# Asking for three summary spreads on ScalarE's queue instead of SyncE's, in a fused block attention and MLP kernel

## Chip, cores, metric

The kernel runs on one core of one Trainium2 chip. The metric is the device time of one execution in microseconds. Before the change it is 621.44 us, the median of three runs (621.18 to 622.95).

## What is computed

Attention over a window and over block summaries, then a two-layer MLP, all in float32:

```python
block, window = (32, 16)
k_sum = k.reshape(B, H, nb, block, D).max(axis=3)
v_sum = v.reshape(B, H, nb, block, D).mean(axis=3)
scores_l = scale * q @ k^T, kept where |i - j| < window
scores_s = scale * q @ k_sum^T + log(block)
a = softmax over both together
x = a @ concat(v, v_sum)
h = x @ w_in
out = (h * erf(softplus(h))) @ w_out
```

q, k and v are 4 batches x 8 heads x 768 positions x 64; w_in is 512 x 2048, w_out 2048 x 512.

## The kernel before

**Tiling.** The 3072 tokens go in 6 chunks of 512. A chunk's attention is done in four quads, one for each pair of heads. A quad has 8 blocks of 64 query positions, and each block sees 96 keys of its window and 24 summaries of its batch, 120 columns in all. So the tile of values of a quad has 120 rows: rows 0 to 95 hold the window's values, and rows 96 to 119 the 24 summary values, the same for all 8 blocks.

**Parts of a quad.** `scores` multiplies queries by keys and summary keys; `softmax` takes the maximum, the exponentials (ScalarE, L606) and the norm (L626, on ScalarE for the fourth quad); `transp` turns the probabilities on TensorE (L637) and ScalarE copies them back into the tile ptr (L642); `av` multiplies them with the tile of values (L663, the value product); `xsplit` stores the result as a high part xh (a cast, L278) and a low part xl (VectorE, L679).

**The MLP.** `mm1` (L766) multiplies xh and xl by a block of w_in that was split in the same way: a cast on ScalarE (L278, "w<-a"), the low part on VectorE (L353). Ahead of that `convert` puts together the raw block rw in three VectorE steps (L331, L334, L337), the first of which needs the block's transfer to have landed. The first quads of the first chunk use the blocks in their order: rw_298 is the first block of w_in, rw_362 the second, and then a third and a fourth; two blocks of w_out follow. `mm2` is the second layer (L917, L921).

**The first chunk.** The first four quads belong to one batch, so its summary values are computed once: `vsum_first` sums the values on TensorE (L502), and ScalarE copies the sums into the tile vsum (L505). From there the 24 rows must be spread over rows 96 to 119 of each quad's tile of values, vwf, 8 times over. For the first quad ScalarE does this with a copy (L278, "vwf<-vsum"). For the other three it is a transfer (L510, "vwf<-vsum", 24 x 8 x 128), which this text calls the first, second and third spread; they serve the second, third and fourth quad. Rows 0 to 95 come from memory (L493, "vwf<-v_win"), the window transfers.

**What sets the order.** Every operation is entered in a `Plan` with its engine, an estimated time, and what it reads and writes. `order` sorts the operations with due times and a long table of corrections (TUNE), and the program emits them in that order; each engine then runs its own instructions strictly one after the other, and waits at the first whose inputs are not there. Before the change SyncE asks for every load and spread.

**Counters.** The arrival of transfers is counted on eight counters, DMAHW0 to DMAHW7 in the rows below. They are dealt out in turn to the transfers as these are written in the program, whatever engine asks, and a transfer is asked for only when the one before it on the same counter has landed.

Of the kernel before, what the change touches and what calls it, by code (L numbers as in the profile page):

```python
# [23 lines left out]
NP = H // 2  # L24
T = 512
SB = S // 64
NB = T // 64
NI = NB // 2
NT = T // 128
NS = 24  # L30
LW = 96
NK = LW + NS
# [19 lines left out]
def f32(ap):  # L52
    return ap.bitcast(F32)
# [127 lines left out]
def bfloat16(x):  # L181

    n = np.array([x], np.float32).view(np.uint32)
    return float(((n + 0x8000) & 0xFFFF0000).astype(np.uint32).view(np.float32)[0])
# [3 lines left out]
def block_attention_mlp(ctx: ExitStack, tc: tile.TileContext, q_t, k_nat, k_win, v_tok, v_nat, v_win, w_in, w_out, out):  # L188
    nc = tc.nc
# [7 lines left out]
    def sb(shape, dtype, name, tag=None):  # L197

        n = math.prod(shape[1:])
        if n % 128 == 0:  # L200
            return pool.tile(shape, dtype, name=name, tag=tag or name)
        t = pool.tile([128, -(-n // 128) * 128], dtype, name=name, tag=tag or name)[0:shape[0], 0:n]
        return t if len(shape) == 2 else t.rearrange("p (a b) -> p a b", a=shape[1]) if len(shape) == 3 else t.rearrange("p (a b c) -> p a b c", a=shape[1], b=shape[2])

    def ps(name, tag):
        return psum.tile([128, 512], F32, name=name, tag=tag)
# [28 lines left out]
    for i in range(3):  # L235
        c = bfloat16(rest)
# [20 lines left out]
    vsum = sb([NK, NP, 128], F32, "vsum")  # L257
# [7 lines left out]
    def pe(us, fn, r=(), w=(), **kw):  # L265
        return P.add({"PE": us}, lambda e: fn(), r, w, **kw)

    def on(us, fn, r=(), w=(), **kw):
        return P.add(us, lambda e: fn(engines[e]), r, w, **kw)

    def act(us, fn, r=(), w=(), **kw):
        return P.add({"ACT": us}, lambda e: fn(), r, w, **kw)

    def dma(kb, fn, r=(), w=(), hold=2.0, **kw):
        return P.add({"SP": max(0.45, kb / 350.0)}, lambda e: fn(), r, w, hold=hold, **kw)

    def copy(e, o, i):
        e.copy(o, i) if e is nc.scalar else e.tensor_copy(o, i)  # L278
# [5 lines left out]
    units = [(kind, g, r) for kind, g in UNITS for r in range(2)]  # L284
    tiles, raws, whl, w32, wide = {}, {}, {}, {}, {}
# [8 lines left out]
    def slot(n, shape, dtype, name):  # L294
        return sb(shape, dtype, name, f"w{n}")
# [7 lines left out]
    def frees(n):  # L303

        return [f"w{n}"] + [f"a{2 * g + r}" for g, x in WHOLE.items() if x == n for r in range(2)]
# [11 lines left out]
    def convert(u):  # L317

        w, s, m = f"w{raw_slot(u)}", {}, number(u)
        at_once = u[0] == "i" or u[1] >= NN  # L320
        home = f"gl{u[2]}" if at_once else f"a{m}"

        def a():
            if at_once:
                s["t"] = sb([128, 2, 512], F32, "a32", home)
            else:
                if u[2] == 0:
                    wide[u[1]] = slot(WHOLE[u[1]], [128, 2, 2, 512], F32, "a32s")
                s["t"] = w32[u] = wide[u[1]][:, u[2]]
            s["a"], s["rw"] = s["t"].bitcast(U32), raws.pop(u)  # L330
            nc.vector.tensor_scalar(s["a"], s["rw"][..., 1], 3, 0x3FFFFFFF, op0=ALU.logical_shift_left, op1=ALU.bitwise_and)  # L331

        def b():
            nc.vector.scalar_tensor_tensor(s["a"], s["rw"][..., 0], 29, s["a"], op0=ALU.logical_shift_right, op1=ALU.bitwise_or)  # L334

        def c():
            nc.vector.scalar_tensor_tensor(s["a"], s["rw"][..., 1], 0xC0000000, s["a"], op0=ALU.bitwise_and, op1=ALU.bitwise_or)  # L337

        on({"DVE": 0.6}, lambda e: a(), [w], [home] if at_once or u[2] else frees(WHOLE[u[1]]))
        on({"DVE": 1.13}, lambda e: b(), [w, home], [home])  # L340
        on({"DVE": 1.13}, lambda e: c(), [w, home], [home])
        if at_once:
            split(u, m if u[0] == "i" else FIRST[m], home, lambda: s["t"])

    def split(u, n, home, whole):
        def high(e):
            t = slot(n, [128, 2, 2, 512], F32R, "w")
            whl[u] = t[:, 0], t[:, 1]
            kept[u] = t
            copy(e, whl[u][0], whole())  # L350

        def low(e):
            e.tensor_tensor(whl[u][1], whole(), f32(whl[u][0]), op=ALU.subtract)  # L353
        on({"ACT": 0.94}, high, [home], frees(n))
        on({"DVE": 1.13}, low, [home, f"w{n}"], [f"w{n}"])

    def parts(m, n):
        u = ("o", m // 2, m % 2)
        split(u, n, f"a{m}", lambda: w32[u])
# [111 lines left out]
    kfirst = [kfs[p // 2][:, p % 2] for p in range(NP)]  # L471

    st = {}

    def where(qd):

        ch, p = divmod(qd, NP)
        seqs = {}
        for j in range(NB):
            seqs.setdefault((NB * ch + j) // SB, []).append(j)  # L480
        return ch, p, [(b, slice(js[0], js[-1] + 1)) for b, js in seqs.items()]
# [16 lines left out]
    def vsum_first(bank):  # L498
        def go(t):
            if t == 0:  # L500
                tiles[bank] = ps("vs", bank)
            nc.tensor.matmul(tiles[bank][0:NK], lhsT=pick[:, 20 - 4 * t:140 - 4 * t], rhs=vts[t // 3][:, t % 3], start=(t == 0), stop=(t == 5))  # L502
        for t in range(6):
            pe(0.87, lambda t=t: go(t), [f"vt{t // 3}"], [bank])
        act(0.5, lambda: nc.scalar.copy(vsum[LW:NK], tiles[bank][LW:NK].rearrange("s (p c) -> s p c", p=NP)), [bank], [f"vsum0{p}" for p in range(NP)])  # L505
        for p in range(NP):
            if p == 0:
                on({"DVE": 1.13, "ACT": 0.95}, lambda e: copy(e, st[0]["vw"][LW:NK], vsum[LW:NK, 0:1, :].to_broadcast([NS, NB, 128])), ["vsum00"], ["vwg0"])
            else:
                dma(100, lambda p=p: nc.sync.dma_start(out=st[p]["vw"][LW:NK], in_=vsum[LW:NK, p:p + 1, :].to_broadcast([NS, NB, 128])), [f"vsum0{p}"], [f"vwg{p}"])  # L510


    def load_quad(qd):
# [115 lines left out]
    def transp(qd):  # L629
        s = st[qd]  # L630
        pr = "pr" if qd >= NP else f"pr{qd}"

        def go():
            s["tp"] = [ps(n, n) for n in PA]
            for a in range(2):
                for i in range(NI):
                    nc.tensor.transpose(s["tp"][a][0:NK, i * 128:(i + 1) * 128], s["pr"][:, NI * a + i], ident)  # L637

        def cp():
            s["pt"] = sb([NK, 2, T], F32, "ptr", "pt")  # L640
            for a in range(2):
                nc.scalar.copy(s["pt"][:, a], s["tp"][a][0:NK, 0:T])  # L642
        pe(0.95, go, [pr], PA)
        act(1.1, cp, PA, ["pt"])

# [7 lines left out]
    def av(qd, bank):  # L653
        s = st[qd]
        s["bank"] = bank

        def go():
            xo = s["xo"] = ps("px", bank)
            for j in range(NB):
                o = slice(64 * j, 64 * j + 64)  # L660
                for a in range(2):
                    r = slice(64 * a, 64 * a + 64)
                    nc.tensor.matmul(xo[r, o], lhsT=s["vw"][:, j, r], rhs=s["pt"][:, a, o], start=True, stop=True)  # L663
        pe(1.08, go, ["pt", "vw"] if qd >= NP else ["pt", f"vwf{qd}", f"vwg{qd}"], [bank])
# [304 lines left out]
    for p in range(3):  # L969
        ksum_first(p)  # L970
        scores(p, banks[p])
        softmax(p, banks[p])
    vsum_first("o2")
    ksum_first(3)
    scores(3, banks[3])
# [3 lines left out]
    for p in range(NP):  # L979
        transp(p)  # L980
        av(p, "o2")
        xsplit(p, {"DVE": 0.6, "ACT": 0.48})
        if p:
            for f in range(G):
                mm1(0, f, (p - 1,))
# [29 lines left out]
    def output(n, bank=None):  # L1015
        transp(n)
        av(n, bank or bank_next())
        xsplit(n, xeng)
# [17 lines left out]
    for k in range(NPER):  # L1036
# [27 lines left out]
        elif k < FAST:  # L1064
# [5 lines left out]
            if qa < NQ:  # L1070
                transp(qa)
# [136 lines left out]
```

## Time and profile before

| | |
|---|---|
| median of the runs | 621.44 us |
| the profiled execution | 622.58 us |
| its span | 620.8 us |
| ScalarE busy | 422.3 us, 68% |
| VectorE busy | 424.0 us, 68% |
| DMA, mean over the span | 242 GB/s |
| SyncE's queue (q1) | 36212 packets, 148.95 MB |
| ScalarE's queue (q10) | 576 packets, 0.52 MB |

The span is the time from the first to the last recorded instruction, the profiled execution's own time lies around it. A row of a timeline reads: start, length, engine, line, operation, output<-input, count, and in brackets how long the engine stood idle before it and what released it. SPq and ACTq are the requests for transfers on SyncE's and ScalarE's instruction streams; a request's length is the time the engine needs to describe the transfer, not that of the transfer. A chain of waits is followed back from the last instruction, each time to what released it. In the list of waits, the first name is the operation that waited, the second what it waited for; then the total, the count and the longest.

ScalarE's queue carries only part of the output at the very end: before that, all transfers are SyncE's.

### The profile page before, as it was taken

What the parts mean: (1) busy time and instruction counts of PE and PEld (TensorE: products, weight loads), DVE (VectorE), ACT (ScalarE), POOL (GpSimd) and SP (SyncE); (2) the same over time, 40 slices, a digit from 0 to 9 for tenths busy, and PEclk for the clock granted to TensorE, in tenths of its full rate; (3) what the DMA queues carried; (4) which work ended last, traced back from release to release, by engine and by line L of the source; (5) the groups of instructions that cost most, each with busy time, mean ns of one, the idle gap of its engine ahead of it and who ended that gap; (6) DMA issues with size and microseconds to landing.
All of it is one profiled execution on the core that took longest, in us unless ns stands there. A gap on an engine that the chain in (4) does not pass through costs nothing.

```text
span 620.8 us, 12141 instructions
## 1 busy us (share of the span) xinstructions
PE 612.9 (99%) x4786; PEld 514.4 (83%) x4786; DVE 424.0 (68%) x884; ACT 422.3 (68%) x855; POOL 3.7 (1%) x27
## 2 busy tenths in 40 slices
PE   9999999999999999999999999999999999999997
PEld 5676666888788889989889889899898898899886
DVE  4989999975989886766857646548546556425442
ACT  5869988986879786885866854855756655552450
POOL 2000000000000000000000000000000000000000
PEclk9999999999999999999999999999999999999999
DMA  8999868654784698799767776756786654574612
GB/s 321 256 337 354 287 205 283 250 183 172 247 304 184 236 339 309 244 370 319 240 217 245 234 264 232 257 209 216 266 289 219 225 170 181 210 265 162 246 68 69
DMA packets 36845, 150.25 MB, mean 242 GB/s; under 512 B 3956, under 2 KB 9396, under 8 KB 24244
## 3 DMA queue, kind: packets, MB, share of 16 engines
q1 hardware_dynamic: 36212, 148.95, 69.4%
q8 instruction: 38, 0.62, 0.4%
q10 hardware_dynamic: 576, 0.52, 0.2%
q14 instruction: 19, 0.16, 0.1%
HBM read 124.13 MB, written 23.07 MB: 237 GB/s over the span
## 4 chain that ended last, share of the span: by engine, by line
PE 93%; DMA 6%; SPq 0%; issue 0%; DVE 0%; ACT 0%
PE ops L921 39%; PE hb L807 15%; PE h L766 13%; PE ha L807 11%; PE ops L917 4%; PE px L663 4%; PE pA L566 3%; DMA rw<-w_in 2%; DMA vwf<-vsum 2%; PE pA L637 1%; PE pB L637 1%; DMA vt<-v_tok 1%; PE pB L566 0%; PE vt L460 0%; SPq L485 0%; SPq L486 0%
## 5 line engine op out<-in xcount | busy, mean ns | idle before, releaser
L921 PE MATMUL ops<-w,gh 128*128 128x512 f32 x704 | 232.8, 396 | 0.0
L921 PEld LDWEIGHTS ops<-w,gh 128*128 128x128 f32 x704 | 132.5, 188 | 27.9 <-issue 0.6
L921 PE MATMUL ops<-w,gl 128*128 128x512 f32 x352 | 137.3, 390 | 0.0
L1166 ACT ACT_TABLE_LOAD x87 | 111.6, 1283 | 1.5
L897 DVE TENSOR_TENSOR hc<-wt,hc 128x1024 f32<-128x1024 f32 x44 | 53.3, 1220 | 76.5 <-ACT wt L885 76.5
L766 PE MATMUL h<-xh,w 128*128 128x512 f32 x256 | 88.8, 406 | 0.0
L278 ACT COPY hc<-hb 128x256 f32<-128x256 f32 x61 | 22.7, 373 | 96.2 <-DVE hc L860 47.6
L921 PEld LDWEIGHTS ops<-w,gl 128*128 128x128 f32 x352 | 66.3, 188 | 12.0
L606 ACT ACTIVATE pr<-pr,stats 128x120 f32<-128x120 f32 x160 | 60.9, 383 | 0.2
L766 PEld LDWEIGHTS h<-xh,w 128*128 128x128 f32 x256 | 48.1, 188 | 12.3 <-issue 2.1
L807 PE MATMUL hb<-w,ws 128*128 128x256 f32 x384 | 56.3, 283 | 0.0
L904 DVE TENSOR_TENSOR gl<-hc,gh 128x1024 fp32r<-128x1024 f32 x44 | 53.8, 1222 | 1.6 <-ACT gh L278 0.7
L807 PEld LDWEIGHTS hb<-w,ws 128*128 128x128 f32 x384 | 50.7, 192 | 0.1
L885 ACT ACTIVATE wt<-wt 128x1024 f32<-128x1024 f32 x48 | 50.4, 1061 | 0.4
L766 PE MATMUL h<-xl,w 128*128 128x512 f32 x128 | 49.9, 390 | 0.0
L857 DVE TENSOR_TENSOR hc<-hb,hc 128x256 f32<-128x256 f32 x32 | 13.5, 422 | 37.4 <-PE hb L807 36.4
L278 DVE CAST gh<-hc 128x1024 fp32r<-128x1024 f32 x38 | 26.3, 691 | 18.1 <-PE ops L921 17.1
L873 ACT ACTIVATE wt<-hc 128x1024 f32<-128x1024 f32 x32 | 32.4, 1052 | 0.2
L606 ACT ACTIVATION_READ_ACCUMULATOR pr<-pr,stats 128x1 f32 x160 | 30.0, 187 | 0.0
L917 PE MATMUL ops<-a32s,gw 128*128 128x512 f32 x64 | 29.5, 595 | 0.0
L766 PEld LDWEIGHTS h<-xl,w 128*128 128x128 f32 x128 | 24.1, 188 | 5.6 <-issue 1.2
L807 PE MATMUL ha<-w,ws 128*128 128x256 f32 x192 | 28.3, 283 | 0.0
(162 smaller groups left out, 1033.9 us busy)
## 6 DMA issues: line engine op xcount, KB each, us to landing
w<-dr SPq DMA_DIRECT2D x36, 1024.0 KB
ws<-ds SPq DMA_DIRECT2D x30, 1024.0 KB
kw<-k_win SPq DMA_DIRECT2D x20, 480.0 KB
rw<-w_in SPq DMA_DIRECT2D x8, 1024.0 KB
rw<-w_out SPq DMA_DIRECT2D x8, 1024.0 KB
dr<-w SPq DMA_DIRECT2D x8, 1024.0 KB
ds<-ws SPq DMA_DIRECT2D x8, 1024.0 KB
vw<-v_win SPq DMA_DIRECT2D x20, 384.0 KB
```

Of the source, the lines that this page charges most:

```text
L278: e.copy(o, i) if e is nc.scalar else e.tensor_copy(o, i)
L606: nc.scalar.activation(s["pr"][:, j], s["pr"][:, j] if qd >= MQ else s["sc"][j // NI][:, i * NK:(i + 1) * NK], AF.Exp, scale=-1.0 if qd >= ...
L663: nc.tensor.matmul(xo[r, o], lhsT=s["vw"][:, j, r], rhs=s["pt"][:, a, o], start=True, stop=True)
L766: nc.tensor.matmul(hs[k, f][:, 0:T], lhsT=w[m], rhs=xt[ch, cc][x], start=(cc == 0 and n == 0), stop=(cc == 3 and n == 2))
L807: nc.tensor.matmul(shape, lhsT=w[m], rhs=y[l], start=first and c == 0 and i == 0, stop=c == 1 and i == 2, skip_group_check=True)
L873: nc.scalar.activation(wt[k, n], hc[k, n], AF.Softplus)
L885: act(0.96, lambda n=n: nc.scalar.activation(wt[k, n], wt[k, n], AF.Erf, scale=-1.0 if k < SOFT else 1.0), [s], [s], table=("sig",), after ...
L897: e.tensor_tensor(hc[k, n], wt.pop((k, n)), hc[k, n], op=ALU.mult)
L904: e.tensor_tensor(gs[k, n][1], hc.pop((k, n)), f32(gs[k, n][0]), op=ALU.subtract)
L917: nc.tensor.matmul(os_[ch, t], lhsT=x[0][:, i % 2, t * 128:(t + 1) * 128], rhs=w32["o", g, i // 2][:, i % 2], start=first, stop=last)
L921: nc.tensor.matmul(os_[ch, t], lhsT=x[y][:, i % 2, t * 128:(t + 1) * 128], rhs=w[m], start=first and n == 0, stop=last and n == 2)
L1166: nc.scalar.preload_act_table_set(sets[o["load"]])
```

## The change

The three requests leave SyncE's stream. In the plan an empty operation stands in their place, so that all else is ordered as before. The requests are made on ScalarE: the first behind the copies of the first quad's ptr, the second and third behind the cast of the first block of w_in.

```diff
@@ split()
             copy(e, whl[u][0], whole())
+            if u == units[0]:
+                spread(2)
+                spread(3)
@@ vsum_first()
-        act(0.5, lambda: nc.scalar.copy(vsum[LW:NK], tiles[bank][LW:NK].rearrange("s (p c) -> s p c", p=NP)), [bank], [f"vsum0{p}" for p in range(NP)])
+        def summed():
+            nc.scalar.copy(vsum[LW:NK], tiles[bank][LW:NK].rearrange("s (p c) -> s p c", p=NP))
+            asked.add(0)
+        act(0.5, summed, [bank], [f"vsum0{p}" for p in range(NP)])
...
-                dma(100, lambda p=p: nc.sync.dma_start(out=st[p]["vw"][LW:NK], in_=vsum[LW:NK, p:p + 1, :].to_broadcast([NS, NB, 128])), [f"vsum0{p}"], [f"vwg{p}"])
+
+                dma(100, lambda: None, [f"vsum0{p}"], [f"vwg{p}"])
+
+    def spread(p):
+        assert 0 in asked
+        asked.add(p)
+        nc.scalar.dma_start(out=st[p]["vw"][LW:NK], in_=vsum[LW:NK, p:p + 1, :].to_broadcast([NS, NB, 128]))
@@ transp()
                 nc.scalar.copy(s["pt"][:, a], s["tp"][a][0:NK, 0:T])
+            if qd == 0:
+                spread(1)
```

`asked` only checks, while the program is written, that a spread stands behind the sums and ahead of its use.

SyncE, from the second window transfer on, before the change; rw is a raw block of weights, vwf_124 holds the tiles of values of the first two quads, vwf_125 those of the last two, and in brackets stands what a request waits for:

```order
L493 DMA vwf_124<-v_win 96x1024 [waits DMAHW5_49]
L510 DMA vwf_124<-vsum_109 24x8x128 [waits DMAHW6_49,Activation_49]
L510 DMA vwf_125<-vsum_109 24x8x128 [waits DMAHW7_49]
L314 DMA rw_434<-w_in 128x2048 [waits DMAHW0_49]
L493 DMA vwf_125<-v_win 96x1024 [waits DMAHW1_49]
L314 DMA rw_494<-w_in 128x2048 [waits DMAHW2_49]
L493 DMA vwf_125<-v_win 96x1024 [waits DMAHW3_49]
L510 DMA vwf_125<-vsum_109 24x8x128 [waits DMAHW4_49]
L314 DMA rw_563<-w_out 128x2048 [waits DMAHW5_49,PE_49]
L314 DMA rw_605<-w_out 128x2048 [waits DMAHW6_49,PE_49]
L519 DMA qb_626<-q_t 128x512 [waits DMAHW7_49]
L444 DMA rows_116<-k_nat 128x768 [waits DMAHW0_49]
```

The same stretch with the change, to the second block of w_out:

```order
L497 DMA vwf_124<-v_win 96x1024 [waits DMAHW5_49]
L314 DMA rw_433<-w_in 128x2048 [waits DMAHW6_49]
L497 DMA vwf_125<-v_win 96x1024 [waits DMAHW7_49]
L314 DMA rw_495<-w_in 128x2048 [waits DMAHW0_49]
L497 DMA vwf_125<-v_win 96x1024 [waits DMAHW2_49]
L314 DMA rw_563<-w_out 128x2048 [waits DMAHW3_49,PE_49]
L314 DMA rw_605<-w_out 128x2048 [waits DMAHW4_49,PE_49]
```

The three spreads are gone. The third block of w_in, rw_434 before and rw_433 now, no longer stands behind a request that needs the sums; and since the counters are dealt anew, it has moved from DMAHW0 to DMAHW6.

ScalarE, from the second copy of the first quad's ptr to the copy of the third quad's, before the change; prf are probabilities, xh_482 (xh_483 with the change) is the high part of the second quad's result:

```order
L642 COPY ptr_382<-pB_369 120x512 [waits PE_49]
L606 ACTIVATE prf_123,stats_106<-h0_300,stats_106 128x120 [waits DVE_49]
L606 ACTIVATE prf_123,stats_106<-h0_300,stats_106 128x120 x3
L606 ACTIVATE prf_123,stats_106<-h1_301,stats_106 128x120 x4
L642 COPY ptr_439<-pA_421 120x512 [waits PE_49,Activation_49]
L642 COPY ptr_439<-pB_422 120x512 [waits PE_49]
L278 CAST w_445<-a32_379 128x1024 [waits DMAHW2_49,DVE_49]
L278 CAST xh_482<-px_463 128x512 [waits PE_49]
L642 COPY ptr_491<-pA_452 120x512 [waits Activation_49]
```

And with the change:

```order
L655 COPY ptr_382<-pB_369 120x512 [waits PE_49]
L523 DMA vwf_124<-vsum_109 24x8x128 [waits DMAHW1_49]
L619 ACTIVATE prf_123,stats_106<-h0_300,stats_106 128x120 [waits DVE_49]
L619 ACTIVATE prf_123,stats_106<-h0_300,stats_106 128x120 x3
L619 ACTIVATE prf_123,stats_106<-h1_301,stats_106 128x120 x4
L655 COPY ptr_438<-pA_422 120x512 [waits PE_49,Activation_49]
L655 COPY ptr_438<-pB_423 120x512 [waits PE_49]
L278 CAST w_444<-a32_379 128x1024 [waits DMAHW2_49,DVE_49]
L523 DMA vwf_125<-vsum_109 24x8x128 [waits DMAHW5_49]
L523 DMA vwf_125<-vsum_109 24x8x128 [waits DMAHW6_49]
L278 CAST xh_483<-px_464 128x512 [waits PE_49]
L655 COPY ptr_492<-pA_453 120x512 [waits Activation_49]
```

Three requests came in. The first stands ahead of the exponentials of the fourth quad. The second and third stand between the cast of the first block and the cast of the second quad's xh; they wait for the counters DMAHW5, last used by the second window transfer, and DMAHW6, last used by the third block of w_in.

More of the change, by code (lines that the diff above doesn't have):

```diff
@@ L473, in block_attention_mlp @@
     st = {}
+    asked = set()
     def where(qd):
@@ L657, in go @@
         def go():
+            assert qd >= NP or qd in asked
             xo = s["xo"] = ps("px", bank)
```

## Prediction

> **What bounds the kernel now.** I read the page first, then the chain of waits of the first 60 us, then each engine's timeline there.
>
> ```profile
> PE 612.9 (99%) x4786; PEld 514.4 (83%) x4786; DVE 424.0 (68%) x884; ACT 422.3 (68%) x855; POOL 3.7 (1%) x27
> 9.90 15.35 DMA rw<-w_in
> 25.26 14.56 DMA vwf<-vsum
> 39.97 1.15 PE px L663 x32
> 42.93 8.20 PE h L766 x36
> PEld ops L917 <- issue: 10.3, 43, 0.3
> ```
>
> The first row (busy time by engine) says that TensorE is busy for 99% of the span. The chain (start, length, what) shows where it is not bound by its own work: up to 39.8 us the end hangs on transfers, the second block of w_in (asked for at 9.90, landed at 25.25) and then the third spread (asked for at 25.26, landed at 39.82). From 39.97 on the chain is TensorE alone, and in the list of waits after 43 us TensorE's matmuls don't appear at all; only its weight loads, which run beside them (the last row is the largest: 10.3 us in 43 times). So whatever time the change gains or loses before 43 us arrives at the end undiminished, and nothing later can give it back.
>
> ```profile
> 27.90 1.15 PE L663 MATMUL px<-ptr,vwf 120*64 120x64 f32 x32 [1.05 <-DMA vwf<-vsum]
> 31.05 0.62 PE L766 MATMUL h<-xh,w 128*128 128x512 f32 x2
> 34.01 1.15 PE L663 MATMUL px<-ptr,vwf 120*64 120x64 f32 x32 [0.52 <-ACT prf L626]
> 35.10 0.65 PE L637 MATMUL pA<-ident,prf 128*120 128x128 f32 x4
> 39.97 1.15 PE L663 MATMUL px<-ptr,vwf 120*64 120x64 f32 x32 [1.03 <-DMA vwf<-vsum]
> 43.00 0.39 PE L766 MATMUL h<-xl,w 128*128 128x512 f32 x1
> ```
>
> These are TensorE's rows (in brackets the idle time ahead and what ended it): the value products of the second, third and fourth quad at 27.90, 34.01 and 39.97, idle for 1.05, 0.52 and 1.03 us before them, and between them at 35.10 the fourth quad's transposes. At 31.05 the ninth and tenth matmul of the first layer begin; the tenth, at about 31.3, is the first to read the second quad's xh. The row at 43.00 is the first matmul on the fourth quad's xl, after which nothing waits. Take all three waits away and TensorE wins 2.6 us: that is the most the change could bring.
>
> ```profile
> 20.00:24.00 4.00, 3.55 (x45) 2.29 (x44) 4.00 (x8) 3.95 (x14) 0.00 (x0) 1.00 1.03 248
> 24.00:28.00 4.00, 2.95 (x24) 2.17 (x24) 3.96 (x6) 2.88 (x9) 0.00 (x0) 1.00 1.05 222
> 28.00:32.00 4.00, 4.00 (x46) 3.40 (x46) 2.93 (x6) 2.92 (x6) 0.00 (x0) 1.00 1.02 273
> ```
>
> The stretches (last columns: granted clock 1.00, DMA share, GB/s) show the DMA engines full, 1.02 to 1.05, in all of this stage.
>
> **What the change removes.** SyncE stood still for the summary values:
>
> ```profile
> SPq L510 <- ACT vsum L505: 8.3, 1, 8.3
> 19.95 1.82 SPq L510 DMA_DIRECT2D vwf<-vsum  x2
> 21.82 0.52 SPq L314 DMA_DIRECT2D rw<-w_in  x1
> 27.51 0.80 SPq L314 DMA_DIRECT2D rw<-w_out  x2
> 28.36 0.42 SPq L519 DMA_DIRECT2D qb<-q_t  x1
> 31.91 0.33 SPq L444 DMA_DIRECT2D rows<-k_nat  x1
> 33.78 0.33 SPq L523 DMA_DIRECT2D kw<-k_win  x1
> SPq L523 <- DMA vwf<-v_win: 1.5, 1, 1.5
> 37.80 2.01 SPq L314 DMA_DIRECT2D rw<-w_in  x2
> ```
>
> After 8.3 us of waiting it asked for two spreads (1.82 us) and only then, at 21.82, for the third block of w_in. With the spreads gone that block is asked for at about 11.6 us, ten microseconds sooner (19.95 less the 8.3 of waiting). I give this nothing directly: the engines were full throughout, and the block queued behind the second block (landed 25.25) and the second window transfer. That one is seen in the row at 27.51, whose order row waits for its counter, DMAHW5; the row at 28.36 waits for DMAHW7, the second spread. So two spreads hold the queue for at most 28.36 - 27.51 = 0.85 us, 0.43 each. The real gain of the loads is those 0.85 us, as far as the spreads' bytes don't pass in the same time on the other queue.
>
> **What it adds: a wait on ScalarE.** The order rows show it: the third spread, now on ScalarE, takes counter DMAHW6, whose last user is now the third block of w_in, and waits until that block has landed. The second waits for DMAHW5, the second window transfer. Queued behind both are, in this order, the cast of the second quad's xh, the third quad's ptr copies, the cast of w, the fourth quad's norm, and the rest.
>
> ```profile
> 21.51 0.59 ACT L642 COPY ptr<-pB 120x512 f32<-120x512 f32 x1
> 25.77 1.11 ACT L278 CAST w<-a 128x1024 fp32r<-128x1024 f32 x1
> 29.09 0.59 ACT L278 CAST xh<-px 128x512 fp32r<-128x512 f32 x1 [2.20 <-PE px L663]
> 31.47 2.40 ACT L626 ACTIVATE prf<-prf,stats 128x120 f32<-128x120 f32 x8
> 25.26 0.83 SPq L510 DMA_DIRECT2D vwf<-vsum  x1
> 614.10 0.38 ACTq L947 DMA_DIRECT2D out<-ob  x1
> 31.92 0.69 DVE L331 TENSOR_SCALAR a<-rw 128x1024 uint32<-128x1024 uint32 x1 [1.04 <-DMA rw<-w_in]
> ```
>
> The price of one request: 0.83 us (SyncE's third spread), as 24 x 8 rows need more describing than the 0.38 us of ScalarE's own output request at 614.10; between these I take 0.83, nearest in shape. The first spread goes out after the copy at 21.51, so from 22.10 to 22.95. It shifts the eight exps, the copies and the cast at 25.77 by 0.83, to 26.6; the cast ends at 27.7 and the second quad's product, at 27.90 before, waits for a copy ending at 26.8 and for the window transfer at 27.5. Hidden, but for a few tenths. The second spread waits until 27.5 and goes out by about 28.4; before, ScalarE idled here until 29.09 (2.20 us), which would have covered it.
>
> The third isn't covered. The third block landed at 31.92 (VectorE's row, idle 1.04 until it). When now? With no spread ahead of it: 27.51 + (31.92 - 28.36) = 31.1. With the first two taking their 0.43 each beside it, as before: 31.9. With each taking twice that, up to its 0.83 of issue: 27.51 + 1.66 + 3.56 = 32.7. I take 31.7, near the row that is there, slightly better as the second spread comes in late. Then the request, 0.83, and 0.1 around it: the cast of xh starts at S = 32.6 instead of 29.09, 3.5 us late.
>
> ```profile
> 29.88 0.68 DVE L679 TENSOR_TENSOR xl<-px,xh 128x512 fp32r<-128x512 f32 x1
> 32.53 1.22 DVE L353 TENSOR_TENSOR w<-a,w 128x1024 fp32r<-128x1024 f32 x1
> 34.92 1.23 DVE L337 SCALAR_TENSOR_TENSOR a<-rw,a 128x1024 uint32<-128x1024 uint32 x1
> 37.77 0.69 DVE L331 TENSOR_SCALAR a<-rw 128x1024 uint32<-128x1024 uint32 x1 [1.02 <-DMA rw<-w_in]
> 41.90 0.68 DVE L679 TENSOR_TENSOR xl<-px,xh 128x512 fp32r<-128x512 f32 x1
> 29.57 0.59 ACT L642 COPY ptr<-pA 120x512 f32<-120x512 f32 x1
> 30.52 1.07 ACT L278 CAST w<-a 128x1024 fp32r<-128x1024 f32 x1
> 36.17 1.05 ACT L278 CAST w<-a 128x1024 fp32r<-128x1024 f32 x1 [0.39 <-DVE a L337]
> ```
>
> How that reaches 43.00: VectorE's xl of the second quad (29.88) needs that cast, so 33.25. ScalarE after the cast: copies and w as at 29.09 to 31.47, so the cast of w begins at S + 1.43 = 34.0 and ends at 35.1. VectorE's low part of w (32.53 before) follows at 35.15, 2.62 late; then its three steps keep their spacing (32.53 to 34.92, 2.39, so 37.5; 1.14 more to the xl at 36.06 before, 38.7; 0.61 to the fourth block's first step, 39.3). That step was at 37.77, held there 1.02 us by the fourth block; it is now 1.5 late, and the block has landed. From there to the fourth quad's xl the rows take 41.90 - 37.77 = 4.13: 43.4 instead of 41.9, ending at 44.1, and the matmul of 43.00 starts at 44.2. **+1.2 us.**
>
> TensorE meanwhile: it reaches the second quad's xh at 31.3 and stops until 33.3, goes on with xl at 34.0, and the third quad's product comes at about 35.8 (34.01 before). The fourth quad's norm (31.47 before, 2.40 long) now ends at 37.4, so that its transposes, which began at 35.10, end at about 38; its product comes at 41, since the cast of the third block (36.17 before) waits for VectorE until 38.8 and the ptr copies stand behind it. All of that stays inside the delay of VectorE's row. In one formula: loss = landing of the third block + 0.93 - 31.4, rounded; 31.1 gives +0.6, 32.7 gives +2.2.
>
> **Sum.** -0 (loads, queue full) + 0 (first two requests, covered) + 1.2 (held ScalarE): span 620.8 to 622.0. The profiled execution took 622.58, 1.8 around its span and 1.14 over the median of 621.44; on the median the sum gives 622.6.
>
> **The rule weighed.** The Trainium skill, DMA: Bandwidth & Descriptors, section "Issuing engines are not separate DMA queues", says that requests from several engines run on the same 16 DMA engines and save only the issuing time. The rows agree: with a DMA share of 1.02 to 1.05 there is no free engine to fill, so by it an earlier request brings nothing, as in my sum; were it false, the third block could land well before 31.1 and the loss would turn into the gain of the second rival.
>
> **Rivals.**
> 1. Slower, a small transfer held up by large ones. On SyncE's queue a spread passed in 0.43 us; on ScalarE's its small pieces may have to alternate with the large ones of the loads. Asked for by 22.95, the first spread would then land only when what stands beside it, up to the third block, is through: 31.1 to 31.9 instead of under 27.9. The second quad's product starts at 31.7; without a wait TensorE needs 43.00 - 27.90 - 0.52 - 1.03 = 13.55 us from there to the matmul of 43.00: 45.2, +2.2, median 623.7. It decides once the first spread lands after 30.7 (30.7 + 13.55 = 44.2). For it: the pieces of one spread are 192 short rows against 8 KB rows of w; against it: no row shows it. The Trainium skill, DMA: Bandwidth & Descriptors, "Queues, rings and completion order", states such a round robin by packet; whether a packet is one row or the whole share of an engine, no run here shows.
> 2. Faster, no hold: the third block lands before ScalarE gets there, at 28.4. Then the third window transfer (landed by 33.78, the request that waited for it) and the fourth come up to 0.85 sooner, the waits of 0.52 and 0.85 of 1.03 go: -1.4, median 620.0. Against it: the queue was full, and the block can't overtake what stands ahead of it.
> 3. The change does nothing: the counter waits are met in time and the transfers stay bound by the full engines: 621.4, for which the block would have to land by 30.5.
>
> **How the numbers follow.** Forecast 0.66, rival 1 0.16, rival 2 0.06, rival 3 0.12. A measurement of this kernel tells about 0.3% from no change, 1.9 us. The forecast's own range, +0.6 to +2.2, is above 1.9 in about one case in six (0.11); rival 1 in most (0.13); rival 2 passes -1.9 only with the first wait gone too (0.03, with what I have missed). So slower 0.24, faster 0.03, same 0.73. The range: 2.2 for the upper ends of the forecast and of rival 1, with a few tenths for the median, gives 623.9; below, it takes in half of rival 3, 621.2.
>
> **What would show it.** Right: a wait of ScalarE of about 3 us before the third spread's request, ended by w_in's third block near 31.7; the cast of the second quad's xh near 32.6; TensorE idle about 2 us before 33.3; the matmul of 43.00 at 44.2; the waits of 1.05, 0.52 and 1.03 changed for one. Rival 1: the second quad's product after 30.7, behind a spread. Rival 2: no idle ScalarE there, product of the fourth quad before 39.5. Wrong altogether if TensorE's idle stretch brought its granted clock under 1.00, or if a TensorE wait after 43 us appeared.

## The result, and the profile after

| | before | with the change |
|---|---|---|
| median of the runs beside each other | 621.54 us (621.18 to 623.17) | 629.12 us (627.54 to 630.67) |
| ratio, 95% interval | | 1.0117 [1.0097, 1.0138] |
| profiled execution, and its span | 622.58, 620.8 us | 629.34, 627.6 us |

Slower by 1.2%, above the range. The span grew by 6.8 us, and all of it lies ahead of one row. TensorE's timeline, with the lines moved by the edit (L679 is the value product, L782 the first layer):

```profile
33.46 1.97 PE L679 MATMUL px<-ptr,vwf 120*64 120x64 f32 x32 [5.74 <-issue]
41.83 1.15 PE L679 MATMUL px<-ptr,vwf 120*64 120x64 f32 x32
46.70 1.15 PE L679 MATMUL px<-ptr,vwf 120*64 120x64 f32 x32
49.74 0.39 PE L782 MATMUL h<-xl,w 128*128 128x512 f32 x1
```

The second quad's product comes at 33.46 instead of 27.90 (+5.56), behind an idle stretch of 5.74 us; the two later products no longer wait; and the matmul that stood at 43.00, ahead of which the fourth quad's xl is made, stands at 49.74 (+6.74). From the second quad's product to it, TensorE needs 16.28 us, where the prediction had 13.55 of work. So **+6.74 = 5.56 late - 1.55 of later waits gone (0.52 + 1.03) + 2.73 of slower work.** The last term is seen in the stretches (columns: length, busy time of PE, PEld, DVE, ACT, POOL, then granted clock, DMA share, GB/s):

```profile
28.00:32.00 4.00, 0.00 (x0) 0.00 (x0) 2.26 (x2) 0.00 (x0) 0.00 (x0) 1.00 1.02 306
32.00:36.00 4.00, 2.54 (x34) 2.37 (x35) 0.00 (x0) 0.53 (x2) 0.00 (x0) 0.61 1.04 316
36.00:40.00 4.00, 4.00 (x11) 3.08 (x11) 3.52 (x6) 4.00 (x12) 0.00 (x0) 0.53 1.01 326
40.00:44.00 4.00, 4.00 (x50) 3.32 (x49) 1.95 (x3) 1.23 (x3) 0.00 (x0) 1.00 1.02 368
```

TensorE does nothing from 28 to 32, and when it starts again the granted clock is low. The 0.61 and 0.53 are means of their stretches; in finer ones the clock is 0.50 from 32.90 to 39.72. From 33.46 on TensorE thus works for 6.26 us at half speed, which costs some 3.1 us, near the 2.73. The DMA engines are as full as before, 1.01 to 1.04.

What was the product waiting for? The row names only "issue". Its ptr was copied by 26.50, and ScalarE's requests and copies read (the row at 26.89 takes the second and third request together; the row at 30.72 is the third alone):

```profile
20.05 1.04 ACT L278 COPY vwf<-vsum 24x1024 f32<-24x1024 f32 x1
20.68 1.41 ACTq L523 DMA_DIRECT2D vwf<-vsum  x1
21.11 0.58 ACT L655 COPY ptr<-pA 120x512 f32<-120x512 f32 x1
25.91 0.59 ACT L655 COPY ptr<-pB 120x512 f32<-120x512 f32 x1
26.38 1.07 ACT L278 CAST w<-a 128x1024 fp32r<-128x1024 f32 x1
26.89 4.62 ACTq L523 DMA_DIRECT2D vwf<-vsum  x2
30.72 0.79 ACTq L523 DMA_DIRECT2D vwf<-vsum  x1
35.47 0.58 ACT L278 CAST xh<-px 128x512 fp32r<-128x512 f32 x1 [8.02 <-PE px L679]
```

The first spread was asked for at 20.68. Its completion is in the trace: the last part landed at 33.37, 12.7 us later, and TensorE starts 0.09 after that. In three other executions of the same spread the distance is again 0.09 to 0.10 (33.54 and 33.63, 33.78 and 33.87, 35.92 and 36.02). The second window transfer had landed at 26.87. So **the product waited for the first spread alone.** The second spread landed at 39.80 and the third at 44.06.

The queues show how a spread of 96 KB can take so long: a view of the DMA queues cut into stretches of 2 us, from 24 to 34 us, for each stretch first q1, SyncE's queue, then q10, ScalarE's (packets, MB, share of the 16 engines).

```profile
q1 hardware_dynamic: 120, 0.64, 96.4%
q10 hardware_dynamic: 11, 0.01, 1.7%
q1 hardware_dynamic: 95, 0.49, 95.4%
q10 hardware_dynamic: 64, 0.03, 9.0%
q1 hardware_dynamic: 78, 0.60, 90.1%
q10 hardware_dynamic: 60, 0.03, 7.1%
q1 hardware_dynamic: 134, 0.56, 100.2%
q10 hardware_dynamic: 68, 0.03, 6.8%
q1 hardware_dynamic: 76, 0.53, 94.8%
q10 hardware_dynamic: 56, 0.03, 7.3%
```

q10 passes its first packet at 25.66, 5.0 us after the request began, and then some 60 packets in 2 us and no more, 7 to 9% of the engines, while SyncE's queue passes 95, 78 and 134 of its own in the three stretches from 26 to 32, larger ones: 307 for 192, so a piece of the spread gets its turn after one or two of the loads'. The spread is 24 x 8 = 192 pieces of 512 bytes; at 60 in 2 us that is 6.4 us. Bytes aren't what it pays for: 0.03 MB in 2 us.

### The profile page after: what moved, and what is told of

Its sections match the earlier page's. It is cut to its first block, busy times and chain, and to the rows that moved or that the text cites. A ratio compares the mean times of both kernels' runs of the same rounds, so it can differ in the third digit from the quotient of the medians.

```text
span 627.6 us, 12139 instructions
## 1 busy us (share of the span) xinstructions
PE 615.5 (98%) x4786; PEld 516.6 (82%) x4786; DVE 424.5 (68%) x884; ACT 422.2 (67%) x855; POOL 3.7 (1%) x27
## 4 chain that ended last, share of the span: by engine, by line
PE 93%; DMA 2%; DVE 2%; SPq 1%; issue 1%; ACTq 0%; ACT 0%; DVEq 0%
PE ops L937 38%; PE hb L823 15%; PE h L782 14%; PE ha L823 11%; PE ops L933 4%; PE px L679 4%; PE pA L579 3%; DMA rw<-w_in 2%; PE pA L650 2%; PE pB L650 1%; ACTq L963 0%; SPq L489 0%; DVE a L337 0%; DVE a L334 0%; PE pB L579 0%
## 5 line engine op out<-in xcount | busy, mean ns | idle before, releaser
L937 PEld LDWEIGHTS ops<-w,gh 128*128 128x128 f32 x704 | 132.5, 188 | 27.9 <-issue 0.6
L782 PE MATMUL h<-xh,w 128*128 128x512 f32 x256 | 90.4, 412 | 0.0
L782 PEld LDWEIGHTS h<-xh,w 128*128 128x128 f32 x256 | 49.1, 192 | 12.7 <-issue 2.1
L782 PE MATMUL h<-xl,w 128*128 128x512 f32 x128 | 50.6, 395 | 0.0
L278 ACT CAST xh<-px 128x512 fp32r<-128x512 f32 (+1 forms) x17 | 8.9, 524 | 33.9 <-PE px L679 30.7
L782 PEld LDWEIGHTS h<-xl,w 128*128 128x128 f32 x128 | 24.6, 192 | 5.8 <-issue 1.2
```

Source lines behind the costliest of these rows:

```text
L782: nc.tensor.matmul(hs[k, f][:, 0:T], lhsT=w[m], rhs=xt[ch, cc][x], start=(cc == 0 and n == 0), stop=(cc == 3 and n == 2))
L937: nc.tensor.matmul(os_[ch, t], lhsT=x[y][:, i % 2, t * 128:(t + 1) * 128], rhs=w[m], start=first and n == 0, stop=last and n == 2)
```

## The experiments

The kernel before had medians from 621.5 to 623.0 us on the chips used, so each time is read as a ratio to the runs of before beside it.

**1. Which spread, and what stands on the other queue.** Two mixtures of before and after. `spread` takes the engine as an argument. In the first the first spread stays on SyncE:

```diff
@@ vsum_first()
-                dma(100, lambda: None, [f"vsum0{p}"], [f"vwg{p}"])
+                dma(100, (lambda: spread(1, nc.sync)) if p == 1 else lambda: None, [f"vsum0{p}"], [f"vwg{p}"])
@@ transp()
-            if qd == 0:
-                spread(1)
...
```

> The first spread stays on SyncE at its old place, the second and third are asked for on ScalarE; no counter holds ScalarE here. Theory A: the second quad's product is back near 27.9; the second spread, asked for near 27, lands some 10 us later, so the third quad's product starts near 37 to 38 instead of 34.0 and the clock may fall: 624 to 628. Theory B: without a hold the loss is gone, 621 to 622.

628.05 us, ratio 1.0090 [1.0067, 1.0114]. The second quad is on time (28.69), and the loss has moved to the third. The chain of waits and TensorE's row:

```profile
26.20 12.98 DMA vwf<-vsum
39.32 1.85 PE L677 MATMUL px<-ptr,vwf 120*64 120x64 f32 x32 [5.04 <-DMA vwf<-vsum]
```

The second spread, asked for by ScalarE at 26.20, takes 12.98 us, and here the profile names it as what TensorE waited for, 5.04 us. ScalarE's third request went out at 27.65 without any hold, so the hold can't be the cause here. And the loads ahead of the second spread had been asked for only 3 to 5 us before it (the third block at 21.31, the fourth at 23.44), since SyncE waits for the sums again.

In the second mixture only the first spread is ScalarE's; SyncE asks for the other two and so waits for the sums again, and the loads behind them are asked for from 21.39 on.

```diff
@@ split()
-            if u == units[0]:
-                spread(2)
-                spread(3)
@@ vsum_first()
-                dma(100, lambda: None, [f"vsum0{p}"], [f"vwg{p}"])
+                dma(100, (lambda p=p: spread(p, nc.sync)) if p > 1 else lambda: None, [f"vsum0{p}"], [f"vwg{p}"])
...
```

> Only the first spread is asked for on ScalarE; the second and third stay on SyncE, which waits for the sums as before, so that the third block of w_in is again asked for near 21.8. No counter holds ScalarE. Theory A: the loads queued at 20 us are enough, the first spread lands at 30 to 32 and the second quad's product starts there: 624.5 to 627.5. Theory B: no hold, 621.5. Theory C, the loads that are asked for ten microseconds earlier are what crowds the spread out: they come late again, 621.5 too, with the product near 28.

622.88 us, ratio 1.0025 [0.9996, 1.0054]. The same request as in the change, from the same engine at the same time, and in the profiled execution it passes at once. ScalarE's queue from 20 to 24 and 24 to 26 us, and TensorE's product of the second quad:

```profile
q10 hardware_dynamic: 147, 0.07, 10.3%
q10 hardware_dynamic: 55, 0.02, 10.9%
29.04 1.15 PE L676 MATMUL px<-ptr,vwf 120*64 120x64 f32 x32 [0.91 <-DMA vwf<-v_win]
```

147 packets by 24 us, where the change had none; the spread landed at 27.89, and the product waited for its window transfer (28.90) instead. So ScalarE's queue isn't slow by itself. **What makes it slow is a backlog on the other queue**: in the change the third and fourth block and two windows had been asked for between 11.46 and 20.67, all ahead of the request. How early doesn't decide it: in the first mixture 3 to 5 us were enough for the same wait. Two of the ten runs of this second mixture took 628.72 and 629.03 us, as long as the change; there is no trace of them, so their cause is open.

**2. Pieces or bytes.** The same three requests, at the same places, with the same counters and as many bytes, in 24 rows of 4 KB each instead of 192 of 512 bytes. The rows are taken from the first quad's finished tile, so this kernel leaves out the other quads' own summaries, and it reads another tile than the change:

```diff
@@ spread()
-        nc.scalar.dma_start(out=st[p]["vw"][LW:NK], in_=vsum[LW:NK, p:p + 1, :].to_broadcast([NS, NB, 128]))
+        nc.scalar.dma_start(out=st[p]["vw"][LW:NK].rearrange("s n c -> s (n c)"), in_=vws[0][LW:NK, 0].rearrange("s n c -> s (n c)"))
```

> Each spread moves the same 96 KB as 24 rows of 4 KB instead of 192 of 512 B. It copies the first quad's finished rows, so the second to fourth quads get the first quad's summaries. Theory A, small pieces alternate with the queued loads' large ones: an eighth of the pieces, so the first spread lands before the second window transfer (about 27), the second quad's product starts near 28, the clock stays 1.00; what is left is the wait of ScalarE for the third block (30.7 in the changed kernel), which moves the cast of xh from 29.1 to about 31.2: 621 to 622. Theory B, the held ScalarE is the cause of the loss: the counters are the same, so 629. If the bytes or the queue as such are slow: 629 too, with the product still after 33.

623.68 us, ratio 1.0028 [1.0014, 1.0041]: three quarters of the loss are gone. The queues from 26 to 28 and 28 to 30 us, and TensorE's product of the second quad:

```profile
q10 hardware_dynamic: 31, 0.09, 20.0%
q10 hardware_dynamic: 5, 0.01, 2.1%
30.31 0.88 PE L679 MATMUL px<-ptr,vwf 120*64 120x64 f32 x23 [0.61 <-DVE w L356]
```

The first spread passes in some 3.5 us, 31 of its 36 packets in two. It still begins only some 5 us after the request (21.11), but with an eighth of the pieces it has landed by 30.2. What this pair shows: the time goes by the pieces, far more than by the bytes. In what is left, 0.28%, the second quad's product still comes 2.4 us later than before (30.31 against 27.90), and part of the executions have a dip of the clock of their own (0.57 in the stretch from 24 to 28 us of this profile); runs with the clock at 1.00 lay at 622.7 to 623.1.

**3. The hold and the early loads, each alone.** A kernel in which no spread is a transfer: GpSimd copies the rows, at the place where SyncE had asked for them; `spread` is no longer called.

```diff
@@ vsum_first()
-                dma(100, lambda: None, [f"vsum0{p}"], [f"vwg{p}"])
+                dma(100, lambda p=p: copy(nc.gpsimd, st[p]["vw"][LW:NK], vsum[LW:NK, p:p + 1, :].to_broadcast([NS, NB, 128])), [f"vsum0{p}"], [f"vwg{p}"])
...
```

> The three spreads are no longer transfers: GpSimd copies the 24 rows for the second to fourth quad, 8 times over, at the place where SyncE asked for them before. ScalarE has no request and no hold; SyncE's loads stay asked for as early as with the change. Theory A (the loss comes from small pieces that have to alternate with a backlog of large ones): the second quad's product waits for its window transfer alone, at 27.3 to 27.9, the third's near 33.4, the fourth's at 38 to 39 (bound by the fourth window transfer); the matmul of 43.00 comes at 41.3 to 42; 619.5 to 620.5. If GpSimd's copies take over 3 us each, the third comes too late and the gain goes: 621 to 622. Theory N (loads asked for early bring nothing, as the DMA engines are full): 620.9 to 621.6.

622.78 us, ratio 1.0005 [0.9994, 1.0016]. The loss is gone, but the gain that was expected didn't come, and the second quad's product stands at 28.86. VectorE's timeline says why; GpSimd's three copies ran from 20.06 to 23.56:

```profile
20.36 1.29 DVE L331 TENSOR_SCALAR a<-rw 128x1024 uint32<-128x1024 uint32 x1
21.58 1.01 DVE L626 TENSOR_SCALAR stats<-stats 128x8 f32<-128x8 f32 x1
22.57 2.06 DVE L334 SCALAR_TENSOR_TENSOR a<-rw,a 128x1024 uint32<-128x1024 uint32 x1
20.06 3.50 POOL L278 COPY vwf<-vsum 24x1024 f32<-24x1024 f32 x3 [14.43 <-ACT vsum L507]
```

Before, the same three steps took 0.68, 0.16 and 1.22 us; beside GpSimd they take 1.29, 1.01 and 2.06, together 2.3 us more. From 20 to 44 us VectorE is busy for 23.9 of 24 us, so it is what bounds this kernel.

On this kernel the hold was put alone: behind the cast of the first block of w_in, ScalarE reads one column of the third block.

```diff
@@ split()
+            if u == units[0]:
+                nc.scalar.copy(stats[:, 120:121], raws[units[2]][:, 0, 0, 1:2].bitcast(F32))
```

> The kernel with GpSimd's copies, and on ScalarE, behind the cast of the first block of w_in, a copy of one column of the third block of w_in: ScalarE is held until that block has landed, as by the counter of the third spread's request, but no spread is a transfer. This is the cost of the hold alone. By the formula of the prediction (landing of the third block, 30.3 to 30.7, plus 0.3 for the tiny copy, less 31.4) the matmul of 43.00 comes at 42.2 to 43: 0.3 to 1.2 us over the kernel with the copies alone. Theory B (the hold is what costs the most): over it by 4 or more.

622.83 us, ratio 1.0008 [0.9996, 1.0020]. ScalarE's timeline:

```profile
31.21 0.19 ACT L352 COPY stats<-rw 128x1 f32<-128x1 f32 x1 [3.68 <-DMA rw<-w_in]
31.31 0.58 ACT L278 CAST xh<-px 128x512 fp32r<-128x512 f32 x1
```

It does stand still, 3.68 us until the third block lands, and the cast of xh comes at 31.31 instead of 30.05. The row that answers to 43.00 moves from 42.87 to 42.92. The hold is there and **costs nothing that shows**. This doesn't go beyond the formula, which sees a loss only where the cast starts after 31.4, and VectorE, late by 2.3 us in this kernel, gives it more cover than the change had; but 4 us and more, as theory B would need, are excluded.

And the early loads alone: the same kernel with SyncE waiting for the sums as before.

```diff
@@ vsum_first()
...
+                    if p == 1:
+                        nc.sync.dma_start(out=stats[LW:NK, 121:122], in_=vsum[LW:NK, 1, 0:1])
...
```

> The kernel with GpSimd's copies, and on SyncE, ahead of the third block of w_in, a transfer of 24 single values that waits for the sums as the spreads did before: the loads are asked for as late as before the change (from about 20.5 on instead of 11.5), and the spreads cost no queue. If loads asked for early bring something: 0.4 to 1.4 us slower than the kernel with the copies alone. If the queue is full anyway and only the place matters (theory N): the same within 0.3, as the third block waits for what stands ahead of it.

622.80 us, ratio 1.0008 [0.9997, 1.0019], against 622.78. The third block was asked for at 21.34 instead of 11.61 and landed at 29.51 instead of 30.60. Asking ten microseconds sooner brings no block sooner, as the prediction had it.

**4. The clock.** Twenty-four matmuls on zeros, the kernel's own filler, ahead of the second quad's product in the changed kernel:

```diff
-FILL = {30: 3, 48: 2, 79: 1, 81: 6, 93: 5, 91: 1, 111: 1}
+FILL = {86: 24, 30: 3, 48: 2, 79: 1, 81: 6, 93: 5, 91: 1, 111: 1}
```

> The changed kernel with 24 more filler products on zeros in front of the second quad's value product, where TensorE idles for 5.7 us and its granted clock then shows 0.53 to 0.61. If the fallen clock costs what the rows between that product and the fourth quad's xl show beyond the 13.55 us of work (16.28 - 13.55 = 2.7 us), the time falls by 2.7, to about 626.4, with the product still near 33.5 and the clock at 1.00. If the clock costs nothing that isn't hidden, it stays at 629.

629.48 us, ratio 1.0114 [1.0090, 1.0137]: not the 626.4 that was expected. The profiled execution took 845.88 us and tells nothing of this stage. The same kernel again:

> The changed kernel with 24 matmuls that serve nothing (the kernel's own way to keep TensorE busy) ahead of the second quad's product, where TensorE stood idle for 5.74 us; all else as in the change. It is the same kernel as the earlier one with fillers. Theory K (2.7 us of the loss come from the lower clock after the idle stretch): clock 1.00 from 32 on and the matmul of 49.74 at 47 to 47.5, 626.4 to 627. Theory D (the second and third spread, landing at 39.8 and 44.1, would bind at any clock): clock 1.00, the third quad's product at 39.8 to 41, the fourth's at 44.2 to 46, both idle ahead of it with a spread named, the matmul of 49.74 at 47.2 to 49; 627 to 628.8.

628.77 us, ratio 1.0096 [1.0072, 1.0119]. The clock was 1.00 throughout, but in the profiled execution the sums came 1.3 us late, so that the first spread was asked for at 22.36 and landed at 35.92, and its rows can't be set beside the change's. Then both kernels on one chip:

> The changed kernel once more, on the chip of the other runs of this batch, to have the next run beside it: 1.010 to 1.013 of the kernel before, the second quad's product at 33 to 36, its clock below 0.65 for some 6 us after it.

> The changed kernel with the 24 matmuls that serve nothing, beside the changed kernel on one chip. The profile with them had the clock at 1.00 throughout, and from the second quad's product to the fourth's 11.16 us instead of 13.24, but that execution began with the sums 1.3 us late. Theory K (the lower clock costs 2 to 2.9 us): 0.3 to 0.45% below the changed kernel's time. Theory D (whoever is slowed by the clock would wait for the second and third spread instead): the same within 0.15%.

The change 629.05 us, ratio 1.0101 [1.0082, 1.0120]; with the fillers 628.20, 1.0086 [1.0065, 1.0107]. The intervals overlap; the profiles speak more clearly. TensorE's rows of the change, then of the kernel with fillers:

```profile
33.63 1.98 PE L679 MATMUL px<-ptr,vwf 120*64 120x64 f32 x32 [6.14 <-issue]
49.17 0.39 PE L782 MATMUL h<-xl,w 128*128 128x512 f32 x1
...
33.87 1.15 PE L679 MATMUL px<-ptr,vwf 120*64 120x64 f32 x32 [1.02 <-issue]
47.76 0.39 PE L782 MATMUL h<-xl,w 128*128 128x512 f32 x1
```

The first spread landed at the same time (33.54 and 33.78), and from the product to the row that answers to 43.00 it is 15.54 us at the lowered clock and 13.89 at 1.00, near the 13.55 of the prediction. The clock costs 1.65 us in this pair of profiles, 0.85 in the medians. Theory K expected 2 to 2.9 and isn't borne out in size: the 0.85 are 0.14%, within the 0.15% that theory D allows. So the lost clock is seen in the rows, but how much of it reaches the end is not settled. With the clock at 1.00 the second spread binds next: it landed at 39.60, and the third quad's product began at 39.85 after 0.39 us of idle time.

**5. Without the queue.** Copies by ScalarE at the three places where the change has ScalarE's requests:

```diff
@@ spread()
-        nc.scalar.dma_start(out=st[p]["vw"][LW:NK], in_=vsum[LW:NK, p:p + 1, :].to_broadcast([NS, NB, 128]))
+        nc.scalar.copy(st[p]["vw"][LW:NK], vsum[LW:NK, p:p + 1, :].to_broadcast([NS, NB, 128]))
```

> The change with a ScalarE copy at each of the three places where the change has ScalarE's request: no spread is a transfer, GpSimd does nothing, and VectorE is not slowed by it. Theory V (with the spreads out of the queues, the stretch is bound by VectorE's own steps, which GpSimd's copies made 2.3 us longer): VectorE's rows at 20 to 23 us have their length of before (0.68, 0.16, 1.22), the cast of the second quad's xh comes at 30.4 behind two copies of 1.04, the matmul of 43.00 at 42.3 to 42.6, 0.4 to 0.8 us sooner than before. Theory W (GpSimd's copies cost nothing, something else holds the kernel without spreads): the same as with GpSimd's copies, 43.4 to 43.7.

622.17 us beside 623.01 of before, ratio 0.9990 [0.9978, 1.0001], so a gain of 0.8 us that the interval doesn't quite secure. VectorE's steps at 20 us have their 0.71, 0.19 and 1.24 back, and from the first of them to the row that answers to 43.00 it is 21.51 us instead of 22.51 with GpSimd's copies and 22.65 before.

Last, the third spread back on SyncE's queue, but behind the loads of this stretch, so that ScalarE copies only for the second and third quad (the diff is against the kernel with three copies):

```diff
@@ split()
-                spread(3)
@@ vsum_first()
-                dma(100, lambda: None, [f"vsum0{p}"], [f"vwg{p}"])
+                def third(p=p):
+                    if p == 3:
+                        nc.sync.dma_start(out=st[p]["vw"][LW:NK], in_=vsum[LW:NK, p:p + 1, :].to_broadcast([NS, NB, 128]))
+                dma(100, third, [f"vsum0{p}"], [f"vwg{p}"])
...
```

> The first and second spread as ScalarE copies, the third as SyncE's own request, behind the fourth window transfer, where it asks after all the loads of this stretch and holds none of them up. By theory A a spread on the same queue as the loads lands right behind what stands ahead of it: 37.9 to 38.5, in time for the fourth quad. ScalarE is free a copy sooner: the cast of xh at 29.4 to 29.6, the first step of the third block at 30.9 (landed 30.6), of the fourth at 36.3 (landed 36.2), the matmul of 43.00 at 41.5 to 41.9: 1.0 to 1.5 us sooner than before. If the third spread lands after 39.9, nothing is gained.

621.56 us beside 623.01 of before, ratio **0.9978 [0.9968, 0.9989]**: 1.4 us faster than before, 7.5 faster than the change on the same chip. SyncE's and TensorE's rows:

```profile
20.45 0.98 SPq L519 DMA_DIRECT2D vwf<-vsum  x1
28.12 1.09 PE L681 MATMUL px<-ptr,vwf 120*64 120x64 f32 x30
33.66 1.15 PE L681 MATMUL px<-ptr,vwf 120*64 120x64 f32 x32
38.53 1.15 PE L681 MATMUL px<-ptr,vwf 120*64 120x64 f32 x32
41.57 0.39 PE L784 MATMUL h<-xl,w 128*128 128x512 f32 x1
```

On the loads' own queue the third spread lands at 38.06, 0.84 behind the fourth window transfer (37.22), in time; none of the three products waits, and the row of 43.00 stands at 41.57.

## Why the prediction was wrong

- **The frame held.** What is lost ahead of 43.00 arrives at the end undiminished: 6.74 at that row, 6.8 in the span, and no TensorE matmul waits after 43 us in the list of waits.
- **The loads held.** The third block was asked for at 11.46 (11.6 predicted) and landed at 30.7, a little ahead of the 31.1 to 32.7 that were given; the gain of that was nothing, as the sum had it.
- **The step that failed is "+ 0 (first two requests, covered)".** It priced the request, 0.83 us of ScalarE, and took the landing from before: a transfer asked for at 22.10 would be there by 27.9. The request was covered indeed; it even ran beside ScalarE's copies (1.41 us from 20.68, beside the copies at 20.05 and 21.11). The landing was not: 33.37. The 0.43 us that a spread took on SyncE's queue was the price of its place in one queue, and said nothing of a second queue beside a full one.
- **The forecast's own term, the hold, was there and was nearly free.** ScalarE's third request waited until the third block had landed and ended at 31.51, but the cast of xh was waiting for the second quad's product until 35.47 anyway. In the run with large rows it shows with its size: the product ended at 31.46, the third request at 31.73, and the cast of xh began at 31.77, 0.3 us late. The formula isn't at odds with that: with the block at 30.7, 30.7 + 0.93 - 31.4 gives 0.2. The 1.2 came from a landing taken a microsecond too late; in the change itself even the 0.2 is hidden.
- **Rival 1 was the right mechanism, given 0.16 and sized too low.** It let the first spread land with the third block, 31.1 to 31.9. The spread isn't tied to a block: its pieces pass at some 60 in 2 us for as long as the other queue has work, so 192 of them, begun at 25.66, need until about 32. The spread lands in twelve parts: eleven came from 31.80 to 32.61 and the last at 33.37, after the third block (30.70) and the third window (32.64). With the product at 33.46, its own sum (13.55 us on) gives 47.0, +4.0.
- **The rest is the clock**, which the prediction named as what would make it wrong altogether: 2.73 us beyond those 13.55 in the profiled execution, 1.99 in the second one, and 0.34 with the fillers. In the medians the fillers gave back 0.85.
- **The rule weighed** (the Trainium skill, DMA: Bandwidth & Descriptors, "Issuing engines are not separate DMA queues", by which several issuers only save issuing time) is right on the bandwidth, 1.01 to 1.04 throughout, and misled on the order: the same request of ScalarE landed at 27.89 or at 33.37, by what stood on the other queue. The round robin by packet of its section "Queues, rings and completion order" is what the rows show, but in turns of about a row. Each of the twelve parts ends with a packet of 4 bytes; the first of these passes at 30.97, 5.3 us after the first piece, and eleven have passed by 31.84, so no part had its whole share in one turn. Without the backlog (the second mixture) the first part was through 0.9 us after the first piece.

Not settled: why q10 passes its first packet only some five microseconds after the request when there is a backlog (4.8 to 5.5 in six profiles, 1.7 in the second mixture); why two runs of that mixture took as long as the change; and, with the packets recorded per queue and not per engine, what exactly one of them alternates with.

## What to carry to other kernels

Before a small transfer moves to another engine's queue, count its pieces and look at what is outstanding on the queue it leaves: in a stretch with full DMA engines it gets a share per piece, beside all the large loads that had been asked for ahead of it. Either it stays in the loads' queue, at the place where it is needed, or it stops being a transfer. And cover is counted to the landing, not to the end of the request.

## What the runs showed that was not expected

- A request by ScalarE doesn't wait for the end of the copies that stand ahead of it: the first started at 20.68 and the second at 26.89, while the copies ahead of them, at 21.11 and 21.59, and the cast at 26.38 (1.07 us) were still to be done or running. So "strictly one after the other", as it is put in the section on the kernel before, doesn't hold for a request behind a copy.
- A load is there only when the last of its 16 parts is, and that one can be far behind. Of the third block's parts in the change, fourteen had landed by 26.96, the others at 28.25 and 30.70; in the last kernel above all sixteen came between 27.04 and 29.88. The prediction counts by the last part alone.
- Copies by GpSimd slow VectorE: three of its steps took 4.36 instead of 2.06 us beside 3.50 us of GpSimd. The Trainium skill, Advanced Engine Details and Errata, "Mode Summary", has them share a port; these rows agree.
- The granted clock doesn't fall at the start of an idle stretch: TensorE was idle from 27.7 on, and the clock fell to 0.50 only at 32.90, for 6.83 us. After 5.04 us of waiting (the first spread on SyncE) it was 0.50 from 39.50 on for 3.41 us. The 6.83 is twice the 3.41. The Trainium skill, TensorE: Matmul & The Clock Gate, "What's actually happening", has the clock halved after an idle window of about 3.4 us; the long waits agree. Short gaps don't decide it by length alone: after 1.61 us it fell, to a mean of 0.57 in its stretch (the spread in large rows), after 1.58 us it stayed at 1.00 (GpSimd's copies with late loads).
